# Three rotating PSUM bank pairs for gate and up, tails in batches of three, down projection in phases, and a last v tile of 128 columns

## The chip, the cores and the metric

The kernel runs on one core of one Trainium2 chip. The metric is the device time of one execution in microseconds. A core has five engines that run side by side, each with its own instruction queue: TensorE (PE; its weight loads are shown as PEld), VectorE (DVE), ScalarE (ACT), GpSimd (POOL) and SyncE (SP), which here issues all DMAs. Matmul results go to PSUM, which has eight banks of 512 fp32 values per partition; all eight are in use, before and after.

## What is computed

The input x has 2048 rows of 576 bf16 values. Two kinds of layers, A and B, are applied in turn, twice each, all with the same weights and with a residual sum:

```python
x = x + A(layernorm(x)); x = x + B(layernorm(x))
x = x + A(layernorm(x)); x = x + B(layernorm(x))

# A: 32 heads of 18; each position sees itself and the 7 before it, 2 apart
q, k, v = split(x @ wqkv)
logits  = sum_d(q[s] * k[s - 2*w]) * 18**-0.5        # w = 0..7
o[s]    = sum_w(softmax(logits)[w] * v[s - 2*w]);  A = o @ wo

# B: F = 4608, no nonlinearity
h = (x @ w_gate) * (x @ w_up);                     B = h @ w_down
```

## The kernel before, in words

**Tiles.** The rows are worked in 18 steps (`seq`, lines 737 to 744): two groups of 1024 rows, in each group all of layer pair 0 and then all of layer pair 1. The first four steps have 128 rows (`nst` = 1), the other fourteen 256 rows (`nst` = 2). Each step calls `attention` (layer A and the normalisation for B) and `glu` (layer B).

**Gate and up.** `glu` cuts the 4608 columns into 36 blocks of 128 (`ft`). A unit is as many blocks as fill a PSUM bank: two blocks in a 256-row step (18 units), four in a 128-row step (9 units). 576 = 4 x 128 + 64, so a unit's gate needs 8 (or 16) full matmuls with 128 contraction rows (`full`, line 649, matmul in line 654) and tails with the remaining 64 rows (`tails`, line 659, matmul in line 665). Gate tails lie on partitions 0 to 63 and up tails on 64 to 127, so that a gate tail and an up tail run as a pair at the same time on the two halves of the array. There are two bank pairs `pg`/`pu`. Units go in batches of two: gate and up of the first unit, the tails of both, gate and up of the second. `evac` (line 672) lets ScalarE copy the gate bank (line 676) and VectorE multiply the up bank with it (line 677) into `h`, which frees the pair.

**Down.** `down` (line 687) multiplies `h` with `w_down` blocks (`wd`, two blocks per 288 KB load, six buffers) into the accumulator banks `acc` (512 columns, one bank per 128 rows, line 693) and `acct` (the remaining 64 columns, line 695), over all 36 blocks. The down matmuls of a batch are emitted after the next batch's gate and up. `finish` adds the accumulators to x on VectorE (lines 727, 729), in the last layer into `ob`, which is stored.

**Attention.** `head` normalises and transposes (on TensorE in the first five steps, by DMA later); `project` (line 396, matmul in line 406) computes q and k, then v, in two bank pairs taken from the same pool as gate and up. The 576 columns of each of q, k, v are stored as 4 tiles of 128 and a remainder of 64; the remainders of q and k make one tile of 128 columns, that of v one of 64. Products with k and v shifts, sums and the softmax run on VectorE (lines 502 to 601), partly on ScalarE; the softmax weights go out to DRAM and back in four copies (`a_dram`, `ab`).

**Order.** No engine order is written by hand. `Plan.op` records each operation with a cost and what it reads and writes; `Plan.run` (line 69) then takes again and again the operation that can start earliest, ties by `prio`, and emits it. `hold`, `pair`, `need` and `free` hand out bank pairs ("unit"): a batch or a projection starts only when as many pairs are free as it needs. All gate, up, tail and down operations are one chain (`bb`, line 644), in the order in which `glu` builds them. A load into `wd` waits for those readers of its buffer that were recorded before it. The plan builds the loads of a batch before the down of the batch before it; in a 128-row step that is eight tiles in flight over six buffers, in a 256-row step four.

Of the kernel before, what the change touches and what calls it, by code (L numbers as in the profile page):

```python
# [132 lines left out]
def kernel(  # L133
# [32 lines left out]

    NXS, NWD, NH, NXB = 4, 6, 4, 3

# [11 lines left out]
    def sb(name, shape, dt=BF16):  # L180
        return consts.tile(shape, dt, name=name)
# [46 lines left out]

    banks = {"pa": [pa[:]], "boot": [acc[:, 0, :], acc[:, 1, :], acct[:]]}
    pool = {"k": "boot"}  # L230

    class Bank:
        made = 0

        def __init__(self):
            Bank.made += 1
            self.key, self.use, self.pool = f"pa{Bank.made}", {}, pool["k"]

        def __call__(self):
# [8 lines left out]
    def dma(dst, src):  # L248
        return lambda: nc.sync.dma_start(dst, src)
# [127 lines left out]
    def attention(j, la, t0, nst):  # L377
# [15 lines left out]
        def bank(p_, u):  # L393
            return (pg, pu)[p_][u["slot"]]
# [59 lines left out]
        if nst == 2:  # L454
# [10 lines left out]
            uv = [(b_, e, 1024 + P * (2 * b_ + e), P) for b_ in range(2) for e in range(2)]  # L465
            ut = [(0, 0, 1536, P), (0, 1, 1664, TL)]
            tv = [(0, 1, uv[0]), (1, 1, uv[2]), (0, 1, uv[1]), (1, 0, ut[1]), (0, 0, ut[0]), (1, 1, uv[3])]
            tb = 0
        else:
            uq = [(b_, e, 512 * b_ + P * e, P) for b_ in range(2) for e in range(4)]  # L470
            ut = [(1, 0, 1536, P), (1, 1, 1664, TL)]
            uv = [(0, e, 1024 + P * e, P) for e in range(4)]
            tb = 1
# [157 lines left out]
    def glu(j, t0, nst, last):  # L631
# [27 lines left out]
        def tails(us):  # L659
            def fn():  # L660
                for m, first in zip(us, (False, True)):
                    s_ = units[m]["slot"]
                    for e, ft in enumerate(fts(m)):
                        for r_, ps in ((slice(0, TL), pg[s_]), (slice(TL, 2 * TL), pu[s_])):
                            nc.tensor.matmul(ps[:, e * n:(e + 1) * n], lhsT=wgu_t[r_, ft * P:(ft + 1) * P],  # L665
                                             rhs=xT[r_, KF, 0:n], start=(first and e == 0), stop=not first,
                                             skip_group_check=True)
            fl = [ft for m in us for ft in fts(m)]
            bb("PE", 190 + 225 * len(us), fn, r=xk + fkeys("wgt", fl) + fkeys("wut", fl),
               w=[f"{nm}_{j}_{m}" for nm in ("wg", "wu") for m in us], need=units[us[-1]])  # L670
# [15 lines left out]

        def down(u, hs, bl):
            for e, ft in enumerate(fts(u)):
                def fn(e=e, ft=ft):
                    wt = wd[bl[e // 2]]  # L690
                    for i in range(nst):
                        lhs = hb[hs][:, e * n + i * P:e * n + (i + 1) * P]
                        nc.tensor.matmul(acc[:, i, :], lhsT=lhs, rhs=wt[:, e % 2, 0:512],  # L693
                                         start=(ft == 0), stop=(ft == NFT - 1))
                        nc.tensor.matmul(acct[:, i * TL:(i + 1) * TL], lhsT=lhs, rhs=wt[:, e % 2, 512:D],  # L695
                                         start=(ft == 0 and i == 0), stop=(ft == NFT - 1), skip_group_check=True)
                bb("PE", 245 * nst, fn, r=[f"h{hs}", f"wd{bl[e // 2]}"], w=["acc"])

        hsl, wsl, units = {}, {}, {}
        prev = []  # L700
        for u in range(0, nu, 2):
            us = [m for m in (u, u + 1) if m < nu]
            for m in us:
                wsl[m] = [load_wd(m * fpu // 2 + g) for g in range(fpu // 2)]
                units[m] = {}
            kw = dict(pair=tuple(units[m] for m in us))
            full(u, wg, "wg", pg, True, False, **kw)
            full(u, wu, "wu", pu, True, False)
            tails(us)
            hsl[u] = evac(u)  # L710
            if len(us) > 1:
                full(u + 1, wg, "wg", pg, False, True)
                full(u + 1, wu, "wu", pu, False, True)
                hsl[u + 1] = evac(u + 1)
            for m in prev:
                pend.append(lambda m=m: down(m, hsl[m], wsl[m]))
            prev = us
            while pend:
                pend.pop(0)()

        def finish():
            for m in prev:
                down(m, hsl[m], wsl[m])
            b = (t0 // 2) % 2
            dst, dk = (ob[b], [f"ob{b}_{i0 + i}" for i in range(nst)]) if last else (xs_f, fk)
            for i in range(nst):
                op("DVE", 690, lambda i=i: nc.vector.tensor_tensor(dst[:, i0 + i, 0:512], acc[:, i, :], xs_f[:, i0 + i, 0:512], op=ALU.add),
                   r=["acc"] + fk, w=dk, prio=0)
            op("DVE", 290, lambda: nc.vector.tensor_tensor(dst[:, i0:i0 + nst, 512:D], acct[:, 0:nst * TL].rearrange("p (i t) -> p i t", i=nst),
                                                           xs_f[:, i0:i0 + nst, 512:D], op=ALU.add),  # L730
               r=["acc"] + fk, w=dk, prio=0)
            if last:
                op("SP", 600, dma(ov[:, t0:t0 + nst, :], ob[b][:, i0:i0 + nst, :]), r=dk, nbytes=P * nst * D * 2, prio=2)
        pend.append(finish)

    pend = []
    seq = []
# [12 lines left out]
    for j, (l, t0, nst) in enumerate(seq):  # L750
        if l == 0 and j:
            load_x(t0, nst)
        pool["k"] = "pa" if j else "boot"
        attention(j, l, t0, nst)
        glu(j, t0, nst, l == n_al - 1)
    while pend:
        pend.pop(0)()
    with tc.manual_schedule():
        pl.run({"unit": 2, **{k: len(v) for k, v in banks.items()}})
# [28 lines left out]
```

## Time and profile before

| what | us |
|---|---|
| median of 3 runs | 1099.64 (1099.42 to 1101.12) |
| span of the profiled execution | 1098.8 |
| its own time beyond the span | not recorded; the median lies 0.8 above the span |
| PE / DVE / ACT busy | 1072.2 / 736.8 / 373.6 |

In the page, "x" is the number of instructions, and a line of the groups gives line, engine, operation, result and sources, shapes and count, then the busy time in us and the mean duration in ns, then the idle time of that engine just before these instructions with what ended it. In a timeline each line has the start, the duration, and the instruction. Matmuls overlap in their pipeline, so a duration there is longer than the distance to the next start, and the distances are what TensorE's time is made of. "128*64" behind a MATMUL or LDWEIGHTS is the part of the array (rows x columns) that it uses. A stretch of the table of windows is given in us from the span's start.

### The profile page before, as it was taken

The page shows a single profiled execution, that of the slowest core. Times are in us where ns is not written, and L with a number is a line of the kernel's source. Part 1 is how long each engine was busy: PE and PEld are TensorE (multiplying, and loading weights), DVE is VectorE, ACT ScalarE, POOL GpSimd, SP SyncE. Part 2 cuts the span into 40 slices and gives each one's busy share as a digit, 9 for nine tenths or more (in the row PEclk, how much of TensorE's full clock was granted, in tenths as well). Part 3 has the DMA queues.
Part 4 walks back from the last instruction along what each step waited for, and adds up shares of the span by engine and source line. Part 5 has one row for each costly group of instructions (what it writes and reads, how often), then busy time and mean ns, then how long its engine had stood idle before and what let it go on. Part 6 is the DMA issues. An engine that isn't in the chain of part 4 may idle for free.

```text
span 1098.8 us, 25249 instructions
## 1 busy us (share of the span) xinstructions
PE 1072.2 (98%) x10812; PEld 785.8 (72%) x10812; DVE 736.8 (67%) x1289; ACT 373.6 (34%) x768; POOL 5.8 (1%) x26
## 2 busy tenths in 40 slices
PE   5899999999999999999999999999999999999998
PEld 4678878777777777777677777777777777777775
DVE  6687988788798978889797423675767857422222
ACT  7445244342443443133342212315242232212121
POOL 2000000000000000000000000000000000000000
PEclk9899999999999999999999999999999999999999
DMA  8954674453535253353524335243433344434341
GB/s 261 341 149 144 187 190 118 125 127 85 117 89 137 70 107 100 106 151 84 140 71 132 110 89 131 66 123 79 132 90 92 112 86 131 110 91 115 91 116 54
DMA packets 146239, 133.17 MB, mean 121 GB/s; under 512 B 42000, under 2 KB 145488, under 8 KB 146128
## 3 DMA queue, kind: packets, MB, share of 16 engines
q1 hardware_dynamic: 146128, 131.57, 44.2%
q8 instruction: 84, 1.38, 0.5%
q14 instruction: 27, 0.22, 0.1%
HBM read 118.96 MB, written 4.73 MB: 113 GB/s over the span
## 4 chain that ended last, share of the span: by engine, by line
PE 95%; DVE 2%; DMA 1%; ACT 1%; issue 0%; DVEq 0%; SPq 0%
PE pg L654 24%; PE pu L654 23%; PE acc L693 22%; PE pg L406 8%; PE pg L665 7%; PE pu L406 4%; PE pa L613 4%; PE acct L695 3%; DMA xnT_A<-xn 1%; PE pa L517 0%; DVE prod L586 0%; DMA wraw<-in_A_wqkv_dram 0%; DVE oT L601 0%; PE pa L556 0%; PE acct L590 0%
## 5 line engine op out<-in xcount | busy, mean ns | idle before, releaser
L676 ACT CAST g_sb<-pg 128x512 bf16<-128x512 f32 x288 | 168.5, 585 | 510.4 <-PE pu L665 414.3
L677 DVE TENSOR_TENSOR h<-pu,g_sb 128x512 bf16<-128x512 f32 x288 | 195.9, 686 | 209.5 <-ACT g_sb L676 154.2
L693 PE MATMUL acc<-wd,h 128*128 128x512 bf16 x1152 | 306.0, 380 | 0.0
L654 PE MATMUL pg<-xnT_B,wg 128*128 128x256 bf16 (+1 forms) x2592 | 300.8, 261 | 1.0 <-ACT xnT_B L371 1.0
L654 PE MATMUL pu<-xnT_B,wu 128*128 128x256 bf16 (+1 forms) x2592 | 299.3, 261 | 0.0
L654 PEld LDWEIGHTS <-wg 128*128 128x128 bf16 x2592 | 213.1, 98 | 60.2 <-issue 25.8
L654 PEld LDWEIGHTS <-wu 128*128 128x128 bf16 x2592 | 230.9, 98 | 23.5
L695 PE MATMUL acct<-wd,h 128*128 128x64 bf16 x1152 | 222.0, 193 | 0.0
L693 PEld LDWEIGHTS <-h 128*128 128x128 bf16 x1152 | 112.7, 98 | 119.9 <-issue 1.5
L406 PEld LDWEIGHTS <-wqkv 128*128 128x128 bf16 (+1 forms) x1260 | 100.3, 101 | 36.9 <-issue 20.7
L586 DVE TENSOR_TENSOR prod<-vT,ab 128x1280 bf16<-128x1280 bf16 (+1 forms) x127 | 94.1, 742 | 45.4 <-DMA ab<-a_dram 44.3
L502 DVE TENSOR_TENSOR prod<-qT,kT 128x2560 bf16<-128x2560 bf16 (+1 forms) x72 | 95.6, 1331 | 31.1 <-ACT kT L448 30.5
L695 PEld LDWEIGHTS <-h 128*128 128x128 bf16 x1152 | 112.9, 98 | 2.3
L406 PE MATMUL pg<-xnT_A,wqkv 128*128 128x256 bf16 (+4 forms) x720 | 93.0, 269 | 4.4 <-DMA xnT_A<-xn 2.8
L601 DVE TENSOR_TENSOR oT<-oT,prod 128x1280 bf16<-128x1280 bf16 (+1 forms) x119 | 90.9, 764 | 3.4
L665 PE MATMUL pg<-xnT_B,wgu_t 64*128 64x256 bf16 (+1 forms) x648 | 88.0, 260 | 0.0
L665 PE MATMUL pu<-xnT_B,wgu_t 64*128 64x256 bf16 (+1 forms) x648 | 88.0, 260 | 0.0
L406 PE MATMUL pu<-xnT_A,wqkv 128*128 128x256 bf16 (+5 forms) x540 | 71.8, 266 | 0.2 <-issue 0.2
L665 PEld LDWEIGHTS <-wgu_t 64*128 64x128 bf16 x1296 | 47.0, 94 | 31.5 <-issue 26.4
L613 PE MATMUL pa<-wo_p,oT 128*128 128x288 bf16 x310 | 48.2, 286 | 1.4 <-DVE oT L601 1.4
L357 ACT ACTIVATE xn<-xf,nmr,rstd 128x576 bf16<-128x576 f32 x48 | 41.5, 864 | 8.4 <-DVE nmr L351 8.2
L506 DVE TENSOR_TENSOR prod<-prod 128x1024 bf16<-128x1024 bf16 (+1 forms) x68 | 43.3, 637 | 1.1
(89 smaller groups left out, 523.8 us busy)
## 6 DMA issues: line engine op xcount, KB each, us to landing
wd<-in_B_w_down_dram SPq DMA_DIRECT2D x324, 288.0 KB, 3.2
ab<-a_dram SPq DMA_DIRECT2D x52, 128.0 KB, 2.7
wg<-in_B_w_gate_dram SPq DMA_DIRECT2D x6, 768.0 KB, 9.1
wu<-in_B_w_up_dram SPq DMA_DIRECT2D x6, 768.0 KB, 10.7
out_dram<-ob SPq DMA_DIRECT2D x8, 288.0 KB, 2.6
wraw<-in_A_wqkv_dram SPq DMA_DIRECT2D x4, 432.0 KB, 5.7
xb<-in_A_x_dram SPq DMA_DIRECT2D x6, 288.0 KB, 3.2
a_dram<-s SPq DMA_DIRECT2D x13, 128.0 KB, 2.6
```

The costliest lines, as they stand in the source:

```text
L406: nc.tensor.matmul(bank(p_, u)[0:m, e * n:(e + 1) * n], lhsT=wqkv[r_, k, c0:c0 + m], rhs=xnT_A[r_, k, 0:n], start=start, stop=stop, skip_g ...
L502: nc.vector.tensor_tensor(late["prod"][p_ % 2][:, :, :, 0:n], q2, k2, op=ALU.mult)
L506: nc.vector.tensor_tensor(prod[:, :, 0:4:2, 0:n], prod[:, :, 0:4:2, 0:n], prod[:, :, 1:4:2, 0:n], op=ALU.add)
L586: nc.vector.tensor_tensor(js(dst), js(vT[:, :, o0:o0 + n]), abw, op=ALU.mult)
L601: op("DVE", 60 + 3 * n, lambda i_=i_: nc.vector.tensor_tensor(oT[:, :, 0:n], oT[:, :, 0:n], late["prod"][i_ % 2][:, 0, :, 0:n], op=ALU.add ...
L613: nc.tensor.matmul(b()[:, 0:HD], lhsT=oT[:, t, i * P:(i + 1) * P], rhs=wo_p[:, t, hh * HD:(hh + 1) * HD], start=(t == 0), stop=(t == KT - 1))
L654: nc.tensor.matmul(pt[:, e * n:(e + 1) * n], lhsT=w_[:, k, ft * P:(ft + 1) * P], rhs=xT[:, k, 0:n], start=(first and k == 0 and e == 0), s ...
L665: nc.tensor.matmul(ps[:, e * n:(e + 1) * n], lhsT=wgu_t[r_, ft * P:(ft + 1) * P], rhs=xT[r_, KF, 0:n], start=(first and e == 0), stop=not ...
L676: op("ACT", 590, lambda: nc.scalar.copy(g_sb[gs][:, 0:ul], pg[use["slot"]][:, 0:ul]), r=[f"wg_{j}_{u}"], w=[f"g{gs}"], prio=0)
L677: op("DVE", 690, lambda: nc.vector.tensor_tensor(hb[hs][:, 0:ul], pu[use["slot"]][:, 0:ul], g_sb[gs][:, 0:ul], op=ALU.mult), r=[f"wu_{j}_{ ...
L693: nc.tensor.matmul(acc[:, i, :], lhsT=lhs, rhs=wt[:, e % 2, 0:512], start=(ft == 0), stop=(ft == NFT - 1))
L695: nc.tensor.matmul(acct[:, i * TL:(i + 1) * TL], lhsT=lhs, rhs=wt[:, e % 2, 512:D], start=(ft == 0 and i == 0), stop=(ft == NFT - 1), skip ...
```

## The change

- There are three bank pairs instead of two (`NB` = 3). `acc` is gone; its two banks are the third pair. At the start, while the first attention runs, that pair serves as scratch space in place of `acc` (`boot`), and one empty TensorE operation hands it over afterwards.
- Batches have three units: gate and up of the first, gate of the second, the tails of all three, up of the second, gate and up of the third.
- Down goes in phases: 2 phases of 9 units in a 256-row step, 3 of 3 units in a 128-row step. All batches of a phase are built first, then all its down matmuls in one stretch. They take one of the three pairs as accumulator (gate bank for the first 128 rows, up bank for the second) and `acct`. After each phase `settle` adds the sums to x, so there are `h` buffers for nine units (`NH` = 9).
- The loads of a phase are all built ahead of its down. With nine loads over six buffers in a 256-row step, loads seven to nine do not know the readers of the first three and have no wait for them.
- The last layer's sum is written as bf16 over the first half of x's own fp32 rows and stored from there; `ob` is gone.
- The last v tile takes columns 1600 to 1727 instead of 1664 to 1727. Its lower 64 columns are the remainder of k again and are not used; v's remainder comes out on partitions 64 to 127. In a 256-row step this tile goes to the up bank instead of the gate bank, and the six tails form three pairs.

```diff
-    NXS, NWD, NH, NXB = 4, 6, 4, 3
+    NXS, NWD, NH, NXB, NB = 4, 6, 9, 3, 3
...
-    ob = [sb(f"ob{i}", [P, NST, D]) for i in range(2)]
...
-    pg = [psum.tile([P, 2 * CH], FP32, name=f"pg{i}") for i in range(2)]
-    pu = [psum.tile([P, 2 * CH], FP32, name=f"pu{i}") for i in range(2)]
-    acc = psum.tile([P, NST, 512], FP32, name="acc")
+    pg = [psum.tile([P, 2 * CH], FP32, name=f"pg{i}") for i in range(NB)]
+    pu = [psum.tile([P, 2 * CH], FP32, name=f"pu{i}") for i in range(NB)]
...
-    banks = {"pa": [pa[:]], "boot": [acc[:, 0, :], acc[:, 1, :], acct[:]]}
+    banks = {"pa": [pa[:]], "boot": [pg[NB - 1][:], pu[NB - 1][:], acct[:]]}
...
-            ut = [(0, 0, 1536, P), (0, 1, 1664, TL)]
-            tv = [(0, 1, uv[0]), (1, 1, uv[2]), (0, 1, uv[1]), (1, 0, ut[1]), (0, 0, ut[0]), (1, 1, uv[3])]
-            tb = 0
+            ut = [(0, 0, 1536, P), (1, 0, 1600, P)]
+            tv = [(0, 1, uv[0]), (1, 1, uv[2]), (0, 1, uv[1]), (1, 1, uv[3]), (0, 0, ut[0]), (1, 0, ut[1])]
+            tb, vs = 0, slice(0, n)
...
-            ut = [(1, 0, 1536, P), (1, 1, 1664, TL)]
+            ut = [(1, 0, 1536, P), (1, 1, 1600, P)]
...
-                (390, lambda u, d: cp(d, vT[0:TL, KF, HALO:HALO + n], bank(tb, u)[0:TL, n:2 * n]), [f"v4{z}"], 0)]
+                (390, lambda u, d: cp(d, vT[0:TL, KF, HALO:HALO + n], bank(1, u)[TL:P, vs]), [f"v4{z}"], 0)]
...
-                for m, first in zip(us, (False, True)):
+                for m, fg, fu in zip(us, (False, False, True), (False, True, True)):
...
+        def settle(ph, use):
+            fin = last and ph == nph - 1
+            for i in range(nst):
+                dst = xs_f[:, i0 + i, :].bitcast(BF16) if fin else xs_f[:, i0 + i, :]
+                op("DVE", 690, lambda i=i, dst=dst: nc.vector.tensor_tensor(dst[:, 0:512], (pg, pu)[i][use["slot"]][:], xs_f[:, i0 + i, 0:512], op=ALU.add),
+                   r=["acc"] + fk, w=fk, prio=0, free="unit", use=use)
...
+        for ph in range(nph):
+            hsl, wsl = {}, {}
+            mine = range(ph * upp, (ph + 1) * upp)
+            for u in range(ph * upp, (ph + 1) * upp, NB):
+                us = (u, u + 1, u + 2)
+                for m in us:
+                    wsl[m] = [load_wd(m * fpu // 2 + g) for g in range(fpu // 2)]
+                    units[m] = {}
+                full(u, wg, "wg", pg, True, False, pair=tuple(units[m] for m in us))
+                full(u, wu, "wu", pu, True, False)
+                full(u + 1, wg, "wg", pg, True, False, need=units[u + 1])
+                tails(us)
+                hsl[u] = evac(u)
                 full(u + 1, wu, "wu", pu, False, True)
                 hsl[u + 1] = evac(u + 1)
...
+                full(u + 2, wg, "wg", pg, False, True)
+                full(u + 2, wu, "wu", pu, False, True)
+                hsl[u + 2] = evac(u + 2)
+            use = {"left": nst}
+            for m in mine:
+                down(m, hsl[m], wsl[m], ph, use)
+            settle(ph, use)
```

More of the change, by code (lines that the diff above doesn't have):

```diff
@@ L697, in down @@
[L697 to L712, printed above, removed]
+                                         start=(first and i == 0), stop=fin, skip_group_check=True)
@@ new lines, in glu @@
+        units = {}
+        for ph in range(nph):
[11 more added lines that the diff above has]
+                hsl[u] = evac(u)
@@ L713, in glu @@
                 full(u + 1, wu, "wu", pu, False, True)
                 hsl[u + 1] = evac(u + 1)
[L715 to L733, printed above, removed]
@@ L754 @@
         attention(j, l, t0, nst)
+        if j == 0:
+            op("PE", 0, lambda: None, w=list(boot_keys), free="unit", use={"slot": NB - 1})
         glu(j, t0, nst, l == n_al - 1)
-    while pend:
-        pend.pop(0)()
     with tc.manual_schedule():
-        pl.run({"unit": 2, **{k: len(v) for k, v in banks.items()}})
+        pl.run({"unit": NB - 1, **{k: len(v) for k, v in banks.items()}})
 _INS = ['A_x', 'A_wqkv', 'A_wo', 'B_x', 'B_w_gate', 'B_w_up', 'B_w_down']
```

32 lines of the change are left out of this document (22 added, 10 removed).

## The prediction

> **What bounds the kernel now.** I read the page first (busy shares), then busy time by stretch, then the timeline of one gate/up batch.
>
> ```profile
> span 1098.8 us, 25249 instructions
> PE 1072.2 (98%) x10812; PEld 785.8 (72%) x10812; DVE 736.8 (67%) x1289; ACT 373.6 (34%) x768; POOL 5.8 (1%) x26
> ```
>
> ```profile
> 0.00:44.00 44.00, 28.49 (x345) 21.34 (x346) 30.12 (x78) 28.48 (x66) 5.81 (x26) 0.88 0.92 294
> 44.00:550.00 506.00, 499.63 (x5443) 373.70 (x5443) 417.57 (x741) 197.19 (x418) 0.00 (x0) 1.00 0.48 128
> 550.00:960.00 410.00, 410.00 (x3803) 295.45 (x3800) 254.19 (x419) 122.21 (x243) 0.00 (x0) 1.00 0.39 103
> 960.00:1098.80 138.80, 134.04 (x1226) 95.32 (x1224) 34.88 (x53) 25.70 (x44) 0.00 (x0) 0.99 0.33 94
> ```
>
> The columns are stretch, length, then busy time of PE, PEld, DVE, ACT and POOL, granted clock, DMA share, GB/s. From 550 to 960 TensorE is never idle. From 44 to 550 it is idle 6.4 us, although VectorE is busy 83% there. The other idle time is the start (15.5 us) and the end (4.8 us: last residual add and store). So only two things can move the time: what TensorE's own instruction stream takes, and new waits in it. A page that says 98% does not tell whether the busy time is useful; for that, one batch of two units of a 256-row tile:
>
> ```profile
> 601.38 1.04 PE L654 MATMUL pg<-xnT_B,wg 128*128 128x256 bf16 x8
> 602.25 1.04 PE L654 MATMUL pu<-xnT_B,wu 128*128 128x256 bf16 x8
> 603.22 0.28 PE L665 MATMUL pg<-xnT_B,wgu_t 64*128 64x256 bf16 x1
> ...
> 603.56 0.27 PE L665 MATMUL pg<-xnT_B,wgu_t 64*128 64x256 bf16 x1
> 603.56 0.27 PE L665 MATMUL pu<-xnT_B,wgu_t 64*128 64x256 bf16 x1
> 603.76 1.05 PE L654 MATMUL pg<-xnT_B,wg 128*128 128x256 bf16 x8
> ...
> 605.52 0.38 PE L693 MATMUL acc<-wd,h 128*128 128x512 bf16 x1
> ...
> 607.48 0.78 PE L613 MATMUL pa<-wo_p,oT 128*128 128x288 bf16 x5
> ```
>
> Durations overlap here, so I use starts. Eight full matmuls take 602.25 - 601.38 = 0.87 us. The next eight end in the tails (64 contraction rows instead of 128), and the tails start 0.97 us later: 0.10 us is lost on the way in. Four tail pairs at 0.11 us would end at 603.67; the next full matmul starts at 603.76: 0.09 lost on the way out. A round trip between the two array shapes costs 0.19, say 0.20 us, in which TensorE counts as busy. Down for two units takes 607.48 - 605.52 = 1.96 us.
>
> **The change part by part.**
>
> *Tails of three units.* A 256-row tile has 18 units: 9 round trips become 6, in 14 tiles: 42 x 0.20 = 8.4 us. A 128-row tile has 9 units in 5 batches, then 3: 8 fewer in 4 tiles, 1.6 us at the same price. The tails, full matmuls and down matmuls are as many as before, in the same shapes. In the built order the tails of a batch stand together, so nothing splits a round trip.
>
> A rule to weigh: the Trainium skill ("TensorEngine Tiling (Array Packing)", Key Properties) says that a change of tiling mode drains the array, which the lost 0.10 us bears out; another page ("TensorE: Matmul & The Clock Gate", Single matmul latency) puts the fixed part of an isolated warm matmul, drain included, at 166 ns. An estimate by that page would be 100 switches x 0.166 = 16.6 us for this part; the rows decide for 10.0.
>
> *Last v tile 128 wide.* Before, its four full matmuls used 64 columns, which is a shape of its own, and its tail fitted neither partner. First row of v in a 256-row tile to the next full matmuls:
>
> ```profile
> 692.92 1.37 PE L406 MATMUL pg<-xnT_A,wqkv 128*128 128x256 bf16 x9
> 694.02 0.28 PE L406 MATMUL pu<-xnT_A,wqkv 64*128 64x256 bf16 x1
> ...
> 694.56 0.28 PE L406 MATMUL pu<-xnT_A,wqkv 64*128 64x256 bf16 x1
> 694.77 1.05 PE L406 MATMUL pg<-xnT_A,wqkv 128*128 128x256 bf16 x8
> ```
>
> ```profile
> 693.45 0.36 PEld L406 LDWEIGHTS <-wqkv 128*64 128x64 bf16 x4 [0.21 <-issue]
> ```
>
> That is 1.85 us. After: eight full 0.87, way in 0.10, three clean pairs 0.33, way out 0.10: 1.40. So 0.45 x 14 = 6.3 us. The wider load is hidden: matmul time goes by the 256 moving columns. In a 128-row tile:
>
> ```profile
> 65.81 0.22 PE L406 MATMUL pg<-xnT_A,wqkv 64*128 64x128 bf16 x1
> 65.96 0.24 PE L406 MATMUL pu<-xnT_A,wqkv 64*64 64x128 bf16 x1
> 66.13 1.28 PE L406 MATMUL pg<-xnT_A,wqkv 64*128 64x128 bf16 x18
> 67.25 0.73 PE L406 MATMUL pu<-xnT_A,wqkv 128*128 128x128 bf16 x8
> 67.91 0.39 PE L693 MATMUL acc<-wd,h 128*128 128x512 bf16 x1
> ```
>
> From 65.81 to 67.91 is 2.10 us. After: one pair and two single tails 0.17, way out 0.10, 24 full matmuls at 0.0556 (0.89 per 16) 1.33: 1.60. Saved 0.5. Of the three such tiles the first stands ahead of a softmax wait in the start and gains nothing: 1.0 us. The very first tile runs them k by k:
>
> ```profile
> 10.05 0.63 PE L406 MATMUL pg<-xnT_A,wqkv 128*128 128x128 bf16 x4
> 10.48 0.56 PE L406 MATMUL pu<-xnT_A,wqkv 128*128 128x128 bf16 x2
> 10.96 0.61 PE L406 MATMUL pg<-xnT_A,wqkv 128*128 128x128 bf16 x4
> ```
>
> Four take 0.43, the two with the 64-wide one 0.48 where 0.21 would do: 0.27 x 4 = 1.1 us, on the path of the start unless the wait for the weight copies steps in. Between 0 and 1.1; I take 1.0.
>
> *Three pairs and the down phases.* Before, an evacuation hid behind the last batch's down. Now it hides behind the batch's other units. How long it takes, and what stands ahead of it:
>
> ```profile
> 1088.20 1.05 PE L654 MATMUL pg<-xnT_B,wg 128*128 128x256 bf16 x8
> 1088.70 0.69 DVE L677 TENSOR_TENSOR h<-pu,g_sb 128x512 bf16<-128x512 f32 x1 [3.88 <-ACT g_sb L676]
> ...
> 1090.23 0.69 DVE L677 TENSOR_TENSOR h<-pu,g_sb 128x512 bf16<-128x512 f32 x1 [0.83 <-PE pu L654]
> ```
>
> ```profile
> L502 DVE TENSOR_TENSOR prod<-qT,kT 128x2560 bf16<-128x2560 bf16 x56 | 82.8, 1478 | 30.5 <-ACT kT L448 30.5
> L727 DVE TENSOR_TENSOR xf<-acc,xf 128x512 f32<-128x512 f32 x16 | 10.4, 682 | 6.2 <-PE acct L695 6.2
> L459 ACT ACTIVATE qT<-pg 128x512 bf16<-128x512 f32 x28 | 16.7, 597 | 45.1 <-PE pu L406 43.5
> L586 DVE TENSOR_TENSOR prod<-vT,ab 128x1280 bf16<-128x1280 bf16 x98 | 80.1, 817 | 44.3 <-DMA ab<-a_dram 44.3
> wd<-in_B_w_down_dram SPq DMA_DIRECT2D x324, 288.0 KB, 3.2
> ```
>
> Unit 0's product ends 1.2 us after its tails (1089.39 against about 1088.2). TensorE wants its up bank after three stretches of 0.87 plus the next gate, 3.5 us: 2.3 us to spare. Unit 2's product ends 1.0 us after its matmuls and its banks are wanted by the next tails 3.2 us after: 2.2 to spare. The longest single VectorE operation is 1.48 us. One such in front costs nothing, two do. Cost 0.
>
> Down of a phase takes one of the three pairs for 9 x 0.98 = 8.8 us (3 units of a 128-row tile: 2.9). Behind it the sum is added to x: 36 more adds of 0.68 and 22 small ones, 25 to 30 us more on VectorE, none on TensorE. The wait that is new: the third unit's tails of the next batch need that pair, and all of TensorE stands behind them. They come 2.61 + 0.10 + 0.45 = 3.2 us after the down; the adds end after 0.27 + 2 x 0.68 = 1.6, with one long operation in front 3.1. Just hidden. The two projections of a tile now follow each other, and v takes over q's pair: ScalarE's two copies (1.2 us) lie under 0.87 x 3 = 2.6 us.
>
> On SP, nine loads of a 256-row phase go ahead of its down over six buffers. In the built order loads seven to nine wait for the earlier load into their buffer, at most 3.2 us each, not for its reader (so down reads the later weights there), and TensorE has no load to wait for inside a phase. What stands behind them on SP are transposes and the softmax round trip. That VectorE waited 44.3 us for such trips, while TensorE was full from 550 on, says that this is slack. Cost 0, up to 9.6 us at one place.
>
> For double waits where these margins meet I add 1.0 us (between -6.4, the old idle time of 44 to 550 all gone, and +10, half a 0.2 us wait per batch of 96).
>
> **Sum.** 8.4 + 1.6 + 6.3 + 1.0 + 1.0 = 18.3, less 1.0: the span goes from 1098.8 to 1081.5. The profiled execution shows a span of 1098.8; the median of the three runs is 1099.64, 0.8 above it, and I carry that 0.8 over: **1082.3**.
>
> **Rivals.**
> 1. *The loss is not in the round trips* but in each tail (the overlap of pairs). Then only the v tile gains: 8.3 - 1.0, so 1092. The even 0.11 us of the pairs speaks against it. Chance 0.07.
> 2. *Waits eat part*: on average 0.05 to 0.18 us per batch of 96, 1087 to 1098. Chance 0.11, of which 0.03 within 0.2% of before.
> 3. *Slower: the evacuations become the bound* from 44 to 550, where VectorE is 83% busy and gets more to do. If two long operations stand ahead of an evacuation, TensorE waits 2 x 1.48 - 2.2 = 0.76 us. In some 42 batches of that stretch it is 32 us, 1113. It decides from 0.2 us per batch (18.3 / 96). For it: the margins fell from about 3 us (down of 1.96 lay there too). Against it: the planner places by ready times close to the measured ones, and puts at most one operation ahead. Chance 0.08.
> 4. *The clock drops*: at the start four matmuls take 0.43, half speed. If each of 14 tiles had one batch of 6.1 us at half speed, 85 us, 1167. The clock column stands at 1.00 from 44 on with two rotating pairs. The Trainium skill ("TensorE: Matmul & The Clock Gate", A second HAM failure mode: psum-queue depth-cycling) warns of just this, cycling through PSUM banks with micro-idle time; no row of before bears it out. Chance 0.02.
> 5. *More than counted*, the old waits go too: 1075. Chance 0.02.
>
> **How the numbers follow.** The forecast has 0.70 (1076 to 1087). A measurement of this kernel can tell about 0.2% from no change (1097.4 to 1101.8). Faster: 0.70 + 0.07 + 0.08 + 0.02 = 0.87; same 0.03; slower 0.08 + 0.02 = 0.10. The range reaches down over case 5 and up over case 1: 1075 to 1092, leaving out most of 2 and all of 3 and 4.
>
> **What would show it.** Three units share one round trip: tails of six pairs, about 0.86 us from first tail to the next full matmul. PEld rows with 128*64 are gone. From the first v row to the next full ones 1.4 us. TensorE idle from 44 on stays near 6 us and the release of tails by a residual add is absent from the waits. I am wrong if the tails show idle time released by VectorE or ScalarE, if transposes arrive late after the doubled loads, or if the clock falls under 1.00 after 44 us.

## The result and the profile after

The changed kernel takes **1094.6 us** (median of 5 runs, 1093.24 to 1096.25) against 1100.43 for the kernel before on the same chip (5 runs, 1099.42 to 1101.12): ratio 0.994, 95% interval 0.9921 to 0.9959. The forecast was 1082.3 with a range of 1075 to 1092. The direction was right; a third of the gain came. Executions in the chip's slower state (one here, of `wd_pool`) are left out of all times below.

In spans, which is how the forecast was worked out, 1098.8 became 1092.5 where 1081.5 was forecast: 11.0 us are missing. The other 1.3 us of the miss are the offset. Every run after lies 2.1 us above its span (1094.6 against 1092.5), and I had carried over 0.8, from a median of other executions.

The page of the kernel after, first lines:

```profile
span 1092.5 us, 25296 instructions
PE 1057.1 (97%) x10812; PEld 792.8 (73%) x10812; DVE 761.4 (70%) x1347; ACT 364.1 (33%) x768; POOL 5.9 (1%) x26
```

TensorE is busy 15.1 us less, as a shorter instruction stream should make it, but it is idle 35.4 us (1092.5 - 1057.1) where it was idle 26.6. The table of windows tells where, after and then before (columns as in the prediction):

```profile
0.00:45.00 45.00, 26.47 (x363) 21.40 (x364) 30.00 (x78) 29.87 (x69) 5.87 (x26) 0.90 0.93 292
45.00:80.00 35.00, 29.54 (x444) 24.02 (x443) 26.73 (x63) 11.63 (x29) 0.00 (x0) 0.93 0.70 211
80.00:600.00 520.00, 518.31 (x5501) 393.03 (x5499) 434.76 (x765) 195.90 (x417) 0.00 (x0) 1.00 0.43 119
600.00:640.00 40.00, 35.92 (x325) 25.75 (x324) 25.43 (x39) 5.70 (x10) 0.00 (x0) 0.96 0.39 117
```

```profile
0.00:45.00 45.00, 29.17 (x358) 22.03 (x359) 30.36 (x78) 29.48 (x69) 5.81 (x26) 0.89 0.92 293
45.00:80.00 35.00, 31.76 (x517) 26.28 (x516) 26.52 (x62) 13.23 (x35) 0.00 (x0) 1.00 0.68 208
80.00:600.00 520.00, 517.19 (x5385) 382.86 (x5385) 431.42 (x744) 198.86 (x412) 0.00 (x0) 1.00 0.45 120
600.00:640.00 40.00, 40.00 (x367) 28.61 (x365) 18.41 (x34) 9.61 (x18) 0.00 (x0) 1.00 0.37 105
```

Read three numbers of a row together: the length, the PE busy time behind it, and the granted clock, which is the third from the end. Idle time is the length less PE busy, and a mean clock below 1.00 tells that TensorE ran at half speed in a part of the stretch (the rows of the stall below show such a part). Two places stand out: 45 to 80 us (5.5 us idle, clock 0.93) and 600 to 640 (4.1 us idle, clock 0.96), a stretch that was full before. The start, too, is idle for 18.5 us instead of 15.8. TensorE's four longest waits behind 45 us (total, times, longest):

```profile
PE pu L666 <- DVE h L678: 4.2, 2, 4.1
PE pa L518 <- DVE s L512: 2.5, 1, 2.5
PE pa L614 <- DVE oT L602: 1.8, 1, 1.8
PE pu L699 <- DVE h L678: 0.9, 3, 0.5
```

The round trips themselves came as forecast. A batch of three units, and a v tile of a 256-row step:

```profile
1047.20 1.04 PE L655 MATMUL pg<-xnT_B,wg 128*128 128x256 bf16 x8
1048.17 0.28 PE L666 MATMUL pg<-xnT_B,wgu_t 64*128 64x256 bf16 x1
...
1048.73 0.27 PE L666 MATMUL pu<-xnT_B,wgu_t 64*128 64x256 bf16 x1
1048.93 1.05 PE L655 MATMUL pu<-xnT_B,wu 128*128 128x256 bf16 x8
```

```profile
98.94 0.60 PE L407 MATMUL pg<-xnT_A,wqkv 128*128 128x256 bf16 x4
...
100.14 0.27 PE L407 MATMUL pu<-xnT_A,wqkv 64*128 64x256 bf16 x1
100.34 0.39 PE L407 MATMUL pg<-xnT_A,wqkv 128*128 128x256 bf16 x2
```

From the last gate stretch to the first tail 0.97 us, from there to the next full matmul 0.76, and 1.40 for v (forecast: 1.40). For the 0.76 the forecast said about 0.86, but its own prices, six pairs at 0.11 and a way out of 0.10, give 0.76: it had added the whole round trip.

### The profile page after: what moved, and what is told of

Same layout as the page of the kernel before. It is cut to its first block, busy times and chain, and to the rows that moved or that the text cites. A ratio compares the mean times of both kernels' runs of the same rounds, so it can differ in the third digit from the quotient of the medians.

```text
span 1092.5 us, 25296 instructions
## 1 busy us (share of the span) xinstructions
PE 1057.1 (97%) x10812; PEld 792.8 (73%) x10812; DVE 761.4 (70%) x1347; ACT 364.1 (33%) x768; POOL 5.9 (1%) x26
## 4 chain that ended last, share of the span: by engine, by line
PE 88%; DVE 5%; DMA 4%; SPq 1%; issue 1%; ACT 1%; DVEq 0%; ACTq 0%
PE pu L655 21%; PE pg L655 21%; PE pg L699 12%; PE pu L699 10%; PE pg L666 6%; PE pg L407 6%; PE pu L407 4%; PE pa L614 3%; PE acct L700 3%; DMA a_dram<-s 2%; DMA ab<-a_dram 1%; SPq L570 1%; DMA wraw<-in_A_wqkv_dram 1%; DVE h L678 1%; DVE prod L503 1%
## 5 line engine op out<-in xcount | busy, mean ns | idle before, releaser
L677 ACT CAST g_sb<-pg 128x512 bf16<-128x512 f32 x288 | 158.9, 586 | 493.6 <-PE pu L666 359.7
L655 PEld LDWEIGHTS <-wu 128*128 128x128 bf16 x2592 | 225.2, 98 | 40.1 <-issue 16.5
L655 PEld LDWEIGHTS <-wg 128*128 128x128 bf16 x2592 | 230.2, 98 | 28.9 <-issue 1.5
L699 PE MATMUL pg<-wd,h 128*128 128x512 bf16 x648 | 231.9, 382 | 0.0
L699 PE MATMUL pu<-wd,h 128*128 128x512 bf16 x504 | 191.5, 380 | 0.9 <-DVE h L678 0.9
L666 PE MATMUL pu<-xnT_B,wgu_t 64*128 64x256 bf16 (+1 forms) x648 | 79.7, 259 | 4.2 <-DVE h L678 4.2
L407 PE MATMUL pg<-xnT_A,wqkv 128*128 128x256 bf16 (+3 forms) x650 | 79.7, 265 | 2.5 <-ACT xnT_A L372 1.6
L666 PE MATMUL pg<-xnT_B,wgu_t 64*128 64x256 bf16 (+1 forms) x648 | 79.8, 259 | 0.0
L407 PE MATMUL pu<-xnT_A,wqkv 128*128 128x256 bf16 (+3 forms) x610 | 77.2, 266 | 0.1
L709 DVE TENSOR_TENSOR xf<-pg,xf 128x512 f32<-128x512 f32 (+1 forms) x40 | 27.4, 684 | 66.3 <-PE pg L699 58.4
```

The source lines that it names most:

```text
L407: nc.tensor.matmul(bank(p_, u)[0:m, e * n:(e + 1) * n], lhsT=wqkv[r_, k, c0:c0 + m], rhs=xnT_A[r_, k, 0:n], start=start, stop=stop, skip_g ...
L655: nc.tensor.matmul(pt[:, e * n:(e + 1) * n], lhsT=w_[:, k, ft * P:(ft + 1) * P], rhs=xT[:, k, 0:n], start=(first and k == 0 and e == 0), s ...
L677: op("ACT", 590, lambda: nc.scalar.copy(g_sb[gs][:, 0:ul], pg[use["slot"]][:, 0:ul]), r=[f"wg_{j}_{u}"], w=[f"g{gs}"], prio=0)
L699: nc.tensor.matmul((pg, pu)[i][use["slot"]][:], lhsT=lhs, rhs=wt[:, e % 2, 0:512], start=first, stop=fin)
L709: op("DVE", 690, lambda i=i, dst=dst: nc.vector.tensor_tensor(dst[:, 0:512], (pg, pu)[i][use["slot"]][:], xs_f[:, i0 + i, 0:512], op=ALU.add),
```

## The stall at 610 to 626 us

What TensorE waits for at 622 is a chain through four engines. Issues of SyncE, kernel after (start, time that the queue was held, instruction, count):

```profile
597.54 12.34 SPq L250 DMA_DIRECT2D wd<-in_B_w_down_dram  x9
...
610.45 0.46 SPq L567 DMA_DIRECT2D a_dram<-s  x1
615.90 2.70 SPq L570 DMA_DIRECT2D ab<-a_dram  x4
```

VectorE in the same stretch, and TensorE behind it:

```profile
605.86 0.69 DVE L551 TENSOR_TENSOR s<-Lt,zs 128x512 bf16<-128x512 f32 x1
...
620.94 0.83 DVE L587 TENSOR_TENSOR prod<-vT,ab 128x1280 bf16<-128x1280 bf16 x1 [6.82 <-DMA ab<-a_dram]
621.68 0.68 DVE L678 TENSOR_TENSOR h<-pu,g_sb 128x512 bf16<-128x512 f32 x1
```

```profile
622.41 0.27 PE L666 MATMUL pu<-xnT_B,wgu_t 64*128 64x256 bf16 x1 [4.08 <-DVE h L678]
...
622.72 1.40 PE L655 MATMUL pu<-xnT_B,wu 128*128 128x256 bf16 x8
623.92 1.92 PE L655 MATMUL pg<-xnT_B,wg 128*128 128x256 bf16 x8
625.62 1.56 PE L655 MATMUL pu<-xnT_B,wu 128*128 128x256 bf16 x8
627.02 0.38 PE L699 MATMUL pg<-wd,h 128*128 128x512 bf16 x1
```

The softmax weights `s` are ready at 606.5. Their store waits on SyncE until 610.45, because nine loads stand in front: loads seven to nine wait there for the landing of the first three in the same buffers (three waits, 7.7 us together). The trip then takes until 620.9. VectorE takes its work in order, so an evacuation (`h`) waits behind the product that needs `ab`; the tails wait for that evacuation's banks; and when TensorE starts again, eight matmuls take 1.2 to 1.7 us instead of 0.87.

**Theory 1**: loads that wait for loads hold SyncE's queue, and this stall is their price. **Rivals**: 1a, the bytes of the burst slow the trip; 1b, the plan has put the trip too late anyway. **Theory 2**: between 45 and 80 us VectorE is late against the plan (2b: because of the added sums). **Rival 2a**: that stretch is the attention's own chain, in the order that the plan has now given it. **Theory 3**: what the new v tile saves in the 128-row tiles becomes idle time, since other engines set the pace of the start.

## The experiments

All times are medians; the ratio is against the kernel before on the same chip (medians 1100 to 1102).

### The two parts alone

Kernel before with only the v tile's lines (`ut`, `tv`, `tb`/`vs`, `ev_t`):

> The kernel before with the v tile alone 128 wide (two pairs, tails of two, down as before). Theory: the v tile is worth what its rows say (0.45 x 14 + 0.5 x 2 + up to 1.1 = 7.3 to 8.4 us) and the lost time comes with the three pairs and the phases: 1092 to 1093.5, no row of TensorE waiting for a residual product behind 600 us. Rival: the lost time is luck of any new order: 1095 or more, with waits of its own at other places.

Measured: 1096.53, ratio 0.9959 (0.9948 to 0.9971). 4.5 us are gained. The rival's number fits (1095 or more), its reason does not: TensorE has no wait behind 600 us. The first gate's first row shows where the theory's gain went, before and then with the v tile alone:

```profile
44.31 1.05 PE L654 MATMUL pg<-xnT_B,wg 128*128 128x128 bf16 x16 [0.97 <-ACT xnT_B L371]
```

```profile
45.77 1.05 PE L654 MATMUL pg<-xnT_B,wg 128*128 128x128 bf16 x16 [1.12 <-ACT xnT_B L371]
```

From the first gate to the end it is 1054.5 us before (1098.8 - 44.31) and 1048.4 here (1094.2 - 45.77): 6.1 gained, where the rows promise 6.3 for the 14 large tiles and up to 1.0 for small ones. The start lost 1.5 in this execution, which is within what the start scatters (below), and TensorE's shorter work there gained nothing that shows: in both, VectorE's last weight copies begin with the arrival of their data at 12.64 and 12.67, and its first product of the attention at 17.85 and 17.88. That speaks for a start that belongs to VectorE, ScalarE and the weights' arrival (theory 3).

Changed kernel with the old v tile:

```diff
-            ut = [(0, 0, 1536, P), (1, 0, 1600, P)]
+            ut = [(0, 0, 1536, P), (0, 1, 1664, TL)]
...
```

> The changed kernel with the old v tiles (64 wide last tile). Theory: the parts add up, and the 11 us that are missing belong to this part: 1094.6 + 7.3 to 8.4 = 1102 to 1103, slower than the kernel before although 50 round trips are gone. Rival: the order is luck, and without the v tile the stalls fall elsewhere or vanish: 1090 to 1098.

Measured: 1101.23, ratio 0.9995 (0.9986 to 1.0005): 50 round trips fewer and nothing gained, 0.8 us below the theory's 1102 to 1103 and far above the rival's range. The same waits as in the whole change are there (4.2 us on `h`, 2.5 on `s`, 1.9 on `oT`). 0.9959 x 0.9995 = 0.9954, inside the interval of the whole change: the parts add up, and the loss is in this one.

### The loads on SyncE's queue

Loads of `w_down` from GpSimd's queue:

```diff
-            op("SP", 550, dma(wd[b][:], wd_v[g]), ...
+            op("SP", 550, lambda: nc.gpsimd.dma_start(wd[b][:], wd_v[g]), ...
```

> The changed kernel with every load of w_down issued from GpSimd's queue in place of SyncE's; the order on TensorE, VectorE and ScalarE stays the same to the instruction. Theory 1 (the doubled loads hold SyncE's queue and with it the softmax round trip): the wait of VectorE for ab near 614 us (6.82) shrinks to 2 or 3 us, the 4.08 us of TensorE behind it and the half-speed spell go: about 1088.5. Rival 1a (the burst of nine loads slows the transfers themselves, wherever they are issued): the landing of a_dram stays at 5 us and the wait keeps 3 us or more: 1092 to 1094.6. Rival 1b (the plan puts the attention late, SyncE has nothing to do with it): 1094.6.

Measured: 1118.04 (1117.2 to 1126.65), ratio 1.0172 (1.0146 to 1.0198), slower than every case expected. Taken by itself this does not tell theory 1 from 1a, since loads that no longer stand in the trip's queue can run beside the trip instead; no row of this run is used. Hence the reverse, the trip alone on GpSimd's queue:

```diff
-            op("SP", 600, lambda: nc.sync.dma_start(dr[:, 0:W * sq], ...
+            op("SP", 600, lambda: nc.gpsimd.dma_start(dr[:, 0:W * sq], ...
-                op("SP", 600, lambda g=g: nc.sync.dma_start(late["ab"]...
+                op("SP", 600, lambda g=g: nc.gpsimd.dma_start(late["ab"]...
```

> The changed kernel, with only the five transfers of each softmax round trip (a_dram and ab, 13 trips) issued from GpSimd's queue; the loads of w_down stay on SyncE as they are, and the order on TensorE, VectorE and ScalarE is the changed kernel's to the instruction. Theory 1 (SyncE's queue, held by loads that wait for loads, is what delays the trip near 610): a_dram leaves when its data are ready at about 606.5, the 4.08 us wait of TensorE and the half-speed spell behind it are gone: 1088 to 1090. Rival 1a (the transfers themselves are slow beside the burst of loads): still a wait of 2 us or more at 614 to 622, 1092 to 1096. Rival 1d: transfers issued by GpSimd take so much longer that waits appear at other places: 1097 or more.

Measured: 1109.6, ratio 1.0068 (1.0051 to 1.0085). The 4 us stall at 622 is gone, but others come: rival 1d by its number, 1a by its mechanism. The worst of them, by issues of GpSimd, then VectorE, then TensorE, and the landings of what is issued in 362 to 376 us (KB each, median us to landing):

```profile
360.34 2.25 POOL L570 DMA_DIRECT2D ab<-a_dram  x4 [2.32 <-DMA a_dram<-s]
```

```profile
370.10 0.83 DVE L587 TENSOR_TENSOR oT<-vT,ab 128x1280 bf16<-128x1280 bf16 x1 [6.30 <-DMA ab<-a_dram]
```

```profile
373.18 1.87 PE L407 MATMUL pu<-xnT_A,wqkv 128*128 128x256 bf16 x8 [3.64 <-DVE h L678]
```

```profile
wd<-in_B_w_down_dram SPq DMA_DIRECT2D x4, 288.0 KB, 8.4
ab<-a_dram POOLq DMA_DIRECT2D x1, 128.0 KB, 7.9
```

The copy left at once and took 7.9 us beside a burst of nine loads, which SyncE issues from 358.7 to 367.2 us. Over the whole run the median landing of `ab` is 2.9 here and 2.7 from SyncE, so it is the company and not the queue. The Trainium skill ("DMA: Bandwidth & Descriptors", Queues, rings and completion order) says that a DMA engine takes turns between the queues that have work for it; the 7.9 us agree that a queue of one's own is no way past the traffic. In the changed kernel, where one queue holds trips and loads, the slowest of the 52 copies of `ab` took 4.3 us.

The clean test leaves queues and order alone and takes away what the three loads wait for: they go to DRAM that nothing reads, so their units are multiplied with earlier weights.

```diff
+            late_ = nst == 2 and g % 9 >= NWD
+            fn = dma(wd_spare[wd_no["n"] % 9], wd_v[g]) if late_ else dma(wd[b][:], wd_v[g])
-            op("SP", 550, dma(wd[b][:], wd_v[g]), w=[f"wd{b}"], ...
+            op("SP", 550, fn, w=[f"wd{b}"], ...
```

> The changed kernel; the order on all engines is its own to the instruction, and SyncE issues as many transfers of the same bytes, but loads seven to nine of a 256-row phase go to memory off the core that nothing uses (so units seven to nine multiply with the weights of units one to three). These loads have no earlier load of their buffer to wait for. Theory 1 (SyncE's queue is held because a load waits for the landing of the load before it in the same buffer): nine loads take 9 x 0.5 us to issue in place of 12.3, the softmax trip near 606 leaves at once, the 4.08 us wait and its half-speed spell go: 1087 to 1090. Rival 1a (the bytes of the burst are what slows the trip): the trip leaves early and lands late, 1092 to 1097. Rival 1b (the place of the trip in the plan, not the loads): 1094.6.

Measured: **1085.61** (1084.44 to 1087.19), ratio 0.986 (0.9842 to 0.9878), 1.4 us below theory 1's range. Without those loads (`lambda: None` in place of the transfer):

> As the run before it in this list, but the loads seven to nine are left out altogether (units seven to nine multiply with the weights of units one to three), so a quarter of the w_down traffic is gone too. Theory 1 without rival 1a: within 1 us of that run. With rival 1a: faster than that run by 2 us or more, 1085 to 1088, with no landing of the trip over 4 us.

Measured: 1085.47, ratio 0.9856 (0.9839 to 0.9873). So theory 1 holds, and 1b falls; leaving out the bytes as well changes 0.14 us, so the bytes by themselves cost nothing here. SyncE's queue with the loads sent elsewhere:

```profile
603.14 0.38 SPq L251 DMA_DIRECT2D out_dram<-xf  x1
605.38 0.34 SPq L568 DMA_DIRECT2D a_dram<-s  x1
609.48 1.75 SPq L571 DMA_DIRECT2D ab<-a_dram  x4
```

The store leaves when its data are there, 5.1 us earlier; 1.2 of these this execution was ahead anyway (below), 3.9 are the queue. From the store to the first copy it then takes 4.10 us (605.38 to 609.48) instead of 5.45 (610.45 to 615.90), where the held loads are still on their way: that much of rival 1a is in the stall. SyncE's waits for a load's landing behind 80 us are 18.9 us in 5 there; in the changed kernel they were:

```profile
SPq L250 <- DMA wd<-in_B_w_down_dram: 192.4, 80, 4.2
```

Because TensorE's order is the same in both, one instruction can be followed. Two score reductions, in the changed kernel, then with the three loads sent elsewhere:

```profile
600.38 0.41 PE L518 MATMUL pa<-s,Esel 128*32 128x128 bf16 x16
...
705.20 0.41 PE L518 MATMUL pa<-s,Esel 128*32 128x128 bf16 x16
```

```profile
599.19 0.41 PE L519 MATMUL pa<-s,Esel 128*32 128x128 bf16 x16
...
698.00 0.41 PE L519 MATMUL pa<-s,Esel 128*32 128x128 bf16 x16
```

The lead grows from 1.2 to 7.2 us between them: **6.0 us at one place**, of which 4.08 are the wait and some 1.7 the half-speed spell (24 matmuls take 627.02 - 622.72 = 4.30 us instead of 3 x 0.87). The 1.2 us before it stand from the start on and are scatter: six kernels with the same order in the start begin the first gate between 42.0 and 43.6 us. Behind 705 us the lead grows by another 1.1, to the 8.3 us between the spans (1092.5 and 1084.2): in the changed kernel alone TensorE waits 0.16 us at 783.68 and 0.50 at 913.66 for an evacuation, with VectorE's late products with `ab` in front of it (VectorE waits 3.50 and 3.84 us for `ab` there, 2.59 and 3.21 in the other kernel). So 7.1 us of the 8.3 are what the waiting loads cost in these two executions. The medians are 9.0 apart; the rest of that was not followed.

### Whole kernels without the waiting loads

The changed kernel leaves something out: nothing holds loads seven to nine until units one to three have been multiplied. At the stall, the last of nine loads is issued by 609.9 us into six buffers, and the down that reads them begins at 627.02, so units one to three get the weights of units seven to nine. From here on no kernel leaves that out, so these are the times to compare with the kernel before.

Loads seven to nine built behind the down that reads their buffer:

```diff
-                    wsl[m] = [load_wd(m * fpu // 2 + g) for g in range(fpu // 2)]
+                    if m - ph * upp < NWD * 2 // fpu:
+                        wsl[m] = [load_wd(m * fpu // 2 + g) for g in range(fpu // 2)]
...
                 down(m, hsl[m], wsl[m], ph, use)
+                k = m + NWD * 2 // fpu
+                if k in mine:
+                    wsl[k] = [load_wd(k * fpu // 2 + g) for g in range(fpu // 2)]
```

> The changed kernel, but the loads of units seven to nine of a 256-row phase are built behind the down that reads their buffer, so that no load waits for another load's landing in front of the softmax round trip. The plan may change the order at some places. Theory 1: no stall of 4 us behind the loads, and TensorE waits for no load, since a load of 3.2 us has 4.9 us of down in front of it: 1088 to 1090. Rival 1c: the late loads come too late, TensorE waits inside the down for one of them, 24 phases by 0.3 to 1 us: 1096 to 1112.

Measured: **1091.02**, ratio 0.9907 (0.9894 to 0.992), just above the expected 1088 to 1090: the stall at 622 is gone and TensorE waits 0.4 us for a load. It beats both kernels. The same three loads issued by hand behind the down, in the changed kernel's own order:

```diff
+                def fn2(e=e, fn=fn, g=u * fpu // 2 + NWD, b=bl[0]):
+                    fn()
+                    if nst == 2 and e == fpu - 1 and NWD <= g % 9 and g % 9 - NWD == u % upp:
+                        nc.sync.dma_start(wd[b][:], wd_v[g])
```

> The changed kernel whole, with nothing left out: its order on TensorE, VectorE and ScalarE stays as it is to the instruction, but each of loads seven to nine of a 256-row phase is issued right behind the down that reads its buffer (units one to three), in place of ahead of the down. Theory 1 (a load that waits for a load's landing in SyncE's queue is what costs 9 us): near the run with loads off the core, 1085 to 1088, the fastest whole kernel. Rival 1c (SyncE, now waiting for the down, holds transposes and trips as long as before, or TensorE waits for the late loads): 1090 to 1096.

Measured: 1091.71, ratio 0.9909 (0.9895 to 0.9924): rival 1c, in part. TensorE's waits behind 80 us show what came instead:

```profile
PE pg L407 <- DMA xnT_A<-xn: 3.2, 2, 2.4
PE pg L700 <- DMA wd<-in_B_w_down_dram: 1.5, 3, 0.9
PE pg L407 <- ACT g_sb L677: 1.1, 1, 1.1
```

A load that waits for a down now holds the transposes behind it in SyncE's queue. The queue is tight either way: what the waiting loads cost can be moved, but less than half of it was won back without leaving loads out. Three phases of six units, six loads over six buffers:

```diff
-        nph = 2 if nst == 2 else 3
+        nph = 3
```

> The changed kernel with three down phases of six units in a 256-row tile in place of two of nine: six loads over six buffers, so no load waits for another of its phase; 14 more sums on VectorE (1.67 us each, 23 us). Theory 1: no wait of SyncE for a load's landing beyond the 128-row tiles, no 4 us stall behind it; the extra sums cost little, since VectorE has room behind 550 us: 1088 to 1092. Rival 4 (the sums and the pair taken three times per tile cost more than the queue gives back): 1095 to 1103.

Measured: 1093.08 (1089.07 to 1099.16), ratio 0.9931 (0.9904 to 0.9958), between the two expectations, and with too wide a spread to tell it from the changed kernel. SyncE waits 0.3 us in all for a load's landing here; 3.5 us on an evacuation and 4.4 us on `oT` are there instead.

### From 45 to 80 us, and the start

Score reduction and output projection of tiles 1 to 4 planned later, on top of the late loads (the projection's line is changed in the same way):

```diff
+        mw = 3000 if 0 < j < 5 else mg
...
-               r=["sel", "s10", "s11", "s12", "s13"], prio=0, margin=mg, **b1.take())
+               r=["sel", "s10", "s11", "s12", "s13"], prio=0, margin=mw, **b1.take())
```

> The kernel with the late loads, in which the plan puts the score reduction (Esel) and the output projection (wo) of tiles 1 to 4 on TensorE at least 3.0 us behind the time at which it thinks their data ready, in place of 0.5. Theory 2 (between 60 and 77 us these stand too early in TensorE's order, and TensorE waits for a VectorE that is late against the plan): the 5.5 us of idle time and the half-speed spell there shrink: 1086 to 1088 in place of 1091.0. Rival 2a (VectorE bounds that stretch, and whoever waits, waits as long): the idle time moves to the next tile's start or to the evacuations, 1090 to 1093.

Measured: 1104.74, ratio 1.0023 (1.0012 to 1.0034). Worse than either case: the wait went to the second projection, and the plan came out otherwise behind it too (waits of 3.4 us for `xn` at 202 us and of 3.2 us for a load at 275). The row with the longest wait ahead of 75 us:

```profile
69.53 1.36 PE L615 MATMUL pa<-wo_p,oT 128*128 128x288 bf16 x5 [4.63 <-DVE xf L621]
```

One down phase in a 128-row tile, also on top of the late loads:

```diff
-        nph = 2 if nst == 2 else 3
+        nph = 2 if nst == 2 else 1
```

> The kernel with the late loads, but 128-row tiles have one down phase in place of three: two sums per tile less on VectorE (0.69 + 0.29 each, 4 tiles: 7.8 us of VectorE, all before 100 us). Theory 2b (the added sums are what makes VectorE late between 60 and 77 us): idle time there falls by 2 us or more, 1087 to 1089. Rival 2a (the stretch is bound by the attention itself, or by the place of its parts in TensorE's order): 1090 to 1092, or worse, as the one down of 8.8 us keeps a pair for longer.

Measured: 1117.68, ratio 1.0141 (1.0124 to 1.0159). It says little of the sums: 18 loads over six buffers cost TensorE 9.7 us of waits, and other waits (7.4 us for `xnT_A`) are new. The clean form, on top of the loads issued by hand, keeps the order and leaves out only the sums of the first two phases:

```diff
+            skip = nst == 1 and ph < nph - 1
...
-                op("DVE", 690, lambda i=i, dst=dst: nc.vector.tensor_tensor(dst[:, 0:512], ...
+                op("DVE", 690, lambda i=i, dst=dst: None if skip else nc.vector.tensor_tensor(dst[:, 0:512], ...
```

> The run before it in this list, with the sums of the first two down phases of the 128-row tiles left out (so a third of their down is kept); the order of all else is the same to the instruction. Theory 2b (the added sums make VectorE late against TensorE between 60 and 77 us): the waits of 1.85, 0.62, 0.50 and 2.50 us there shrink to the 2.3 us in all of the kernel before, and the half-speed spell goes: 3 to 5 us less than that run. Rival 2a (that stretch is bound by the attention's own chain, in which the new order puts the score reduction and the output projection): within 1.5 us of that run.

Measured: 1091.88, ratio 0.9911 (0.9897 to 0.9924), the same as with them (1091.71). The four waits, in the changed kernel (the hooked loads leave this order as it is), and two of them without the sums:

```profile
64.71 0.79 PE L614 MATMUL pa<-wo_p,oT 128*128 128x288 bf16 x5 [1.85 <-DVE oT L602]
68.11 0.77 PE L614 MATMUL pa<-wo_p,oT 128*128 128x288 bf16 x5 [0.62 <-DVE xf L620]
70.85 0.27 PE L518 MATMUL pa<-s,Esel 128*32 128x64 bf16 x12 [0.50 <-DVE xf L620]
73.62 0.21 PE L518 MATMUL pa<-s,Esel 128*32 128x64 bf16 x4 [2.50 <-DVE s L512]
```

```profile
65.14 0.79 PE L614 MATMUL pa<-wo_p,oT 128*128 128x288 bf16 x5 [1.85 <-DVE oT L602]
...
74.06 0.21 PE L518 MATMUL pa<-s,Esel 128*32 128x64 bf16 x4 [2.50 <-DVE s L512]
```

The two left out here (0.63 and 0.50) agree too, all four to 0.01 us: theory 2b falls. What is left is rival 2a, which no run shows directly: the plan now puts these matmuls between down matmuls and waits on VectorE for the chain in front of them. Before, TensorE had five waits of 3.2 us together in 45 to 80 us, the longest 1.37, and no spell at half speed.

Old v tail in the 128-row tiles only, on top of the late loads (theory 3):

```diff
-            ut = [(1, 0, 1536, P), (1, 1, 1600, P)]
+            ut = [(1, 0, 1536, P), (1, 1, 1664, TL)]
```

> The kernel with the late loads, but the 128-row tiles have their old v tail (64 columns wide); the 256-row tiles keep the new one. Theory 3 (the start is set by weight copies, VectorE and ScalarE, so that what the v tile saves there becomes idle time): no slower than with it, 1089 to 1091.5, and the idle time of TensorE ahead of the first gate is 1.5 to 3 us less. Rival 3 (it is worth its rows there too): 1.6 us slower, 1092.6.

Measured: 1091.77, ratio 0.9914 (0.9898 to 0.9929), against 0.9907 with the new tail everywhere. The difference of 0.75 us lies inside the intervals; idle time ahead of 45 us is 1.2 us less (16.3 against 17.6). The number lies between theory 3's 1089 to 1091.5 and the rival's 1092.6, and theory 3 is the nearer one: of the 2.0 us that the forecast had for the small tiles, under 1 is left, or nothing that can be told.

## Why the prediction was wrong, by its steps

- **Tails of three units (8.4 + 1.6) and v tile (6.3 + 1.0 + 1.0): right in TensorE's stream.** Busy time fell by 15.1, and half speed took 2.9 us more of it than before (busy x (1 - clock) in the windows, as the clock is a mean: after 2.6 + 2.1 + 1.4, before 29.17 x 0.11 = 3.2 in the start), so at full speed the stream is about 18 us shorter; 18.3 was the sum. (Both traces hold 10812 matmuls; the two digits of the clock make this good to some 0.5 us.) From the v part, 6.1 us arrive behind the first gate and nothing sure ahead of it.
- **SyncE: "Cost 0, up to 9.6 us at one place". This is the step that failed.** It cost 6.0 us at one place and 1.1 at two others. Without these waits the time was 1085.61, inside the range. I had seen the waits for each load (taken as 3.2 us at most, which is the median landing; the longest was 4.2) and the softmax trip behind them, and took VectorE's waits of 44.3 us for the trip in the kernel before as slack. They are slack only as long as no evacuation stands behind them in VectorE's order. At 614 one did. The bound was kept out of the sum and, worse, out of the range: 1092 was the price of rival 1 alone.
- **Waits where margins meet, 1.0 us: too small.** In 45 to 80 us TensorE idles 5.5 us instead of 3.2, and half speed costs it 2.1. Together 4.3 us. (Some 0.7 of the 2.1 belong to a spell at the first gate, from 43 to 46.5 us.) In the start it idles 18.5 instead of 15.8, of which the scatter of the first gate, up to 1.6 us between kernels of one order, can be a part. Why the plan's order costs this much before 80 us stays open. I had looked at the margins of evacuations, which held (0.5 us at most in one wait beside the stall), and not at where the plan would put the attention's matmuls in a changed chain.
- **The old idle time of 44 to 550**: as forecast neither gone nor more behind 80 us: 1.7 us idle in 80 to 600 against 2.8.
- **The offset**: 2.1 instead of 0.8.
- **Rivals.** Rival 1 falls with the rows of the round trips. Rival 2 (waits eat part, 1087 to 1098) held the time and had 0.11, but by luck: it spread the waits over 96 batches, and they came in a few stalls. Rival 3 did not come: in steady work no evacuation is the bound, and the sums of the 128-row tiles can be left out with nothing gained. Rival 4 came in small: no stretch of steady work falls to half speed, but some longer waits bring a spell.

Sum of idle time and half speed, by windows, against before: the start 2.1 more (idle 2.7 more, half speed 0.6 less), 45 to 80 us 4.3, 80 to 600 us 1.1 less, 600 to 640 us 5.5 (4.1 + 1.4; from the rows, the 1.4 is 1.7), behind 640 us 0.9. That is 11.7, where the forecast had 1.0 for waits. With the 0.3 that the stream fell short of 18.3 these are the 11.0 us missing in spans, and the offset makes 12.3. So the loads are the largest single loss, and what was lost up to 80 us, 6.4 together, is nearly as much.

## What to carry to other kernels

Count each DMA that waits for another DMA as time of its queue, and follow what stands behind it through every in-order engine until TensorE: slack ends at the first evacuation that is queued behind the late operand. A change of TensorE's stream also moves everything that a planner places, so a shorter stream should be given a range that holds a few stalls of 2 to 4 us, some with a spell at half speed. To prove such a cause, change only where a transfer goes or whether it is issued, keep the order to the instruction, and follow one instruction through both traces.

## What the runs showed of the hardware

- **A wait can cost more than its length.** Behind the 4.08 us wait, matmuls ran at half speed for some 3 us, which took 1.7 us more; behind the 2.50 us wait at 73.62 too, where down pairs start 0.48 us apart instead of 0.24:

```profile
73.77 0.61 PE L699 MATMUL pg<-wd,h 128*128 128x512 bf16 x1
74.24 0.61 PE L699 MATMUL pg<-wd,h 128*128 128x512 bf16 x1
```

  A wait of 2.58 us in the run with the trip on GpSimd's queue was followed by full speed (the next eight matmuls start 0.87 us later):

```profile
426.26 1.03 PE L655 MATMUL pu<-xnT_B,wu 128*128 128x256 bf16 x8 [2.58 <-DVE h L678]
```

  The Trainium skill ("TensorE: Matmul & The Clock Gate", Part 1: The HAM clock gate) puts the drop to half speed behind an idle window of about 3.4 us that runs freely. The 4.08 us, longer than that, agree; the 2.50 us, which follow 0.50 us of idle and a few small matmuls, show that a shorter wait can be enough, and the 2.58 us that it need not be.
- **Another queue is not another road.** A 128 KB copy took 7.9 us beside nine loads, from a queue that held only its own round trip; its median is 2.7 to 2.9.
- **The start scatters**: six kernels with the same order there reach the first gate at 42.0 to 43.6 us.
